# An adaLN transformer block, forward and backward: the work between the two attention loops rearranged (memory sides, halves of the dense gradient, column sums, operand loads)

## Chip, core and metric

The program runs on one core of a Trainium2 chip. The metric is device time in microseconds: the median of three runs of the kernel before is 2784.3 us (2782.75 to 2784.43). A profile records one execution by itself.

## What is computed

One transformer block with adaptive layer norm on x of 2048 tokens by 512 (bf16), its output, and the gradients of nine inputs for a given grad_out:

```python
mod = (_silu(c) @ w_mod).reshape(c.shape[0], 6, 1, -1)
sa, ca, ga, sb, cb, gb = (mod[:, i] for i in range(6))
h = _layernorm(x) * (1 + ca) + sa
x = x + ga * A(h, A_wqkv, A_wo)              # 32 heads of 16, softmax attention
h = _layernorm(x) * (1 + cb) + sb
x = x + gb * B(h, B_w1, B_b1, B_w2, B_b2)    # relu(h w1 + b1)^2 w2 + b2, width 1792
out, vjp = jax.vjp(f, A_x, A_wqkv, A_wo, B_w1, B_b1, B_w2, B_b2, c, w_mod)
return out, *vjp(grad_out)
```

The second line is written shorter here than in the reference.

## The kernel before

Tokens lie in 16 tiles of 128 (TT) or four chunks of 512 (QC); the dense width of 1792 in 14 blocks of 128 (FC) or four quarters of 448 (QF). The queues named SP, ACT and POOL issue DMAs in the order in which their instructions stand; a tile framework decides where each instruction is placed, under data dependences and the buffers of its pools. Products on PE are chained by hand (`pe`), some POOL instructions too (`chain("pool", ...)`). The stages:

- **Start (0 to about 109 us).** Loads of x (SP), wqkv, w_mod (ACT); layer norm; 16 DMA transposes make h1T (L164); q, k, v are projected tile by tile (L236) and stored to scratch memory: `qp_st` and `kp_st` (L251), `va_st` (L255), while POOL makes h1 and stores `h_st`. `prep_weights` (L334) transposes wo, w1 and w2 by DMA into `woT` and two `wbig` tiles and stores these as `w1T_st` and `w2T_st` for later reloads. The pool `wbig` has two buffers of 1792 KB; it is opened after the start's own pools are released.
- **Forward attention (to about 1100 us).** Scores, exponentials on ScalarE (L682) and products with v. Between them a generator `mlp(c, ...)` runs the MLP of chunk c, forward and backward: output projection, second layer norm, `h2T`, first dense layer into `rT` and its square `sT`; token-major copies `tokh` by DMA transposes; gradient of w2 (L486, sums over chunks in `dw2acc`); the dense gradient `ds` from w2T and `gfT` (grad_out transposed, times the gate gb) into `rT`; its transposes, stored to `dztok_st` (L514); gradient of the norm's input `dh` (L525) and the chain through the norm on VectorE and ScalarE (L531 to L555); column sums `sums` on POOL (L537, L538, L557, L611); per token tile the attention's output gradient (L578), stored for the loop, and the block's output (L604).
- **Tail (1100 to 1311 us).** Chunk 3 of the MLP. Wherever it calls `pump(k)`, k pieces of another generator, `fill`, are put in: gradients of wo and of w1 for quarters 0 and 1 (L779), by four-matmul groups, with two PSUM banks `ab0` and `ab1` and four `do` banks. The pieces need dz (the dense gradient, token-major), reloaded by `load_dz`.
- **A phase of its own (about 1251 to 1311).** The pool `bwdw` is opened, weights for the end are transposed (`wqT`), a third of w_mod is loaded, then the other two (`wmod2`); `ops` tiles for the backward loop are zeroed and their 28 loads issued (`load_one`, L905 and L909); gradients of w1 for quarters 2 and 3 (L933, L950) with dz2 and dz3; column sums multiplied out (L940); `mod_grads` for rows 2 to 5.
- **Backward attention loop (1311 to about 2652).** Eight groups of four heads; VectorE L999, ScalarE L985 and L1034, PE L981, L993, L1030, L1042, L1050, L1071.
- **Last stage (to 2769).** dq, dk, dv are turned into dx (L1202, `ln_back`), and the gradient of wqkv (L1211); token-major copies `dtok` come by 12 SP transposes (L1144); `flush_rows` sums rows by PE (L1194); `mod_grads` for rows 0 and 1; outputs go out on SP through `wqblk` (L1216) and `dwmod_sb` (L869).

`mod_grads(pool, wm, j0, j1, part)` makes, for each quarter of the rows of w_mod, one ScalarE product into `dwmod_sb` (one buffer, sent out on SP) and one VectorE product with its sum.

Of the kernel before, what the change touches and what calls it, by code (L numbers as in the profile page):

```python
# [17 lines left out]
BF = dt.bfloat16  # L18
# [15 lines left out]
def kernel(  # L34
# [52 lines left out]
    dcpart = persist.tile([P, 2, DC], F32, name="dcpart")  # L87
# [34 lines left out]
    SP.dma_start(out=wqkv_nat[:], in_=A_wqkv.rearrange("(ic p) j -> p ic j", p=P))  # L122
# [184 lines left out]
    with ExitStack() as ph:  # L307
        wbig = ph.enter_context(tc.tile_pool(name="fwb", bufs=2))
        onb = ph.enter_context(tc.tile_pool(name="f0", bufs=1))
        wkb = ph.enter_context(tc.tile_pool(name="fw0", bufs=2))  # L310

# [51 lines left out]
        def mlp(c, bank, tail=None):  # L363
# [74 lines left out]
            pump(14)  # L438
            for ic in range(DC):
# [11 lines left out]
            for fc in range(FC):  # L451
# [16 lines left out]
                if 2 <= fc < 6:  # L468
                    oc = fc - 2
                    DVE.tensor_scalar(gfT[:, oc, :], gfT[:, oc, :], modcol[:, 5, oc:oc + 1], None, ALU.mult)  # L470
# [4 lines left out]
            pb = bank()  # L475
            for t in range(4):
                pe(PE.matmul(pb[:], ones_bf[:, 0:P], gc[:, t, :], start=(t == 0), stop=(t == 3)))
            if c == 0:
                DVE.tensor_copy(db2acc[:], pb[0:1, :])
            else:  # L480
                DVE.tensor_tensor(db2acc[:], db2acc[:], pb[0:1, :], ALU.add)
            yield
            for fc in range(FC):
                pw = bank()
                for t in range(4):
                    pe(PE.matmul(pw[:], stok[fc // 7][:, t, (fc % 7) * P:(fc % 7 + 1) * P], gc[:, t, :],  # L486
                                 start=(t == 0), stop=(t == 3)))
                if c == 0:
                    DVE.tensor_copy(dw2acc[:, fc, :], pw[:])
                else:  # L490
                    DVE.tensor_tensor(dw2acc[:, fc, :], dw2acc[:, fc, :], pw[:], ALU.add)
                if c == QC - 1:
                    w2blk = wk.tile([P, D], BF, name="w2blk", tag="wb")
                    DVE.tensor_tensor(w2blk[:], dw2acc[:, fc, :], gb_bc, ALU.mult)
                    ACT.dma_start(out=out_6[fc * P:(fc + 1) * P, :], in_=w2blk[:])
                yield

            for fc in range(FC):
                pds = bank()
                for oc in range(DC):  # L500
                    pe(PE.matmul(pds[:], w2T[:, oc * FF + fc * P:oc * FF + (fc + 1) * P], gfT[:, oc, :],
                                 start=(oc == 0), stop=(oc == DC - 1)))
                db1p = wk.tile([P, 1], F32, name="db1p", tag="db1p")
                DVE.scalar_tensor_tensor(out=rT[:, fc, :], in0=pds[:], scalar=2.0, in1=rT[:, fc, :],
                                         op0=ALU.mult, op1=ALU.mult, accum_out=db1p[:])
                DVE.tensor_tensor(db1acc[:, fc:fc + 1], db1acc[:, fc:fc + 1], db1p[:], ALU.add)
                j = fc % 7
                if j == 0:
# [772 lines left out]
```

## Time and profile before

| what | value |
|---|---|
| median of three runs | 2784.3 us |
| the profiled execution | 2770.57 us |
| its span, first to last instruction | 2768.8 us |
| granted TensorE clock, mean | 0.922 of full |
| busy PE, DVE, ACT, POOL | 2270.3, 1838.4, 2275.3, 625.2 us |
| DMA | 466.89 MB, 169 GB/s mean |

Busy us by stage (windows of the trace):

| window | PE | DVE | ACT | POOL | clock | DMA share |
|---|---|---|---|---|---|---|
| 0 to 60 | 22.2 | 32.9 | 19.8 | 43.1 | 0.86 | 0.71 |
| 60 to 120 | 51.8 | 37.0 | 40.0 | 31.5 | 0.94 | 0.96 |
| 200 to 1085 | 719.7 | 368.6 | 854.7 | 169.6 | 0.86 | 0.44 |
| 1100 to 1250 | 119.7 | 82.2 | 25.6 | 37.0 | 0.83 to 0.93 | 0.52 to 1.10 |
| 1250 to 1311 | 32.2 | 24.1 | 9.6 | 24.0 | 0.78 | 0.86 |
| 1311 to 2652 | 1152.5 | 1215.3 | 1217.4 | 285.1 | 0.98 | 0.99 |
| 2652 to 2769 | 97.0 | 54.5 | 21.7 | 22.8 | 0.91 | 0.72 |

A row reads: of the window's length so many microseconds the engine was busy. A clock under 1 means that TensorE was granted less than full speed. A DMA share near 1 means that all 16 DMA engines moved packets all the time.

### The profile page before, as it was taken

To read this page: it belongs to the slowest core of one execution; us is meant where nothing else is said; L and a number is where in the kernel's file an instruction comes from. 1 tells how busy PE (TensorE), PEld (TensorE's weight loads), DVE (VectorE), ACT (ScalarE), POOL (GpSimd) and SP (SyncE) were. 2 spreads that over 40 slices of the span, in tenths; PEclk is the share of its full clock that TensorE was granted. 3 is DMA by queue.
4 is the path that set the end of the run, shared out by engine and by line. 5 is a ranking of instruction groups with operands and counts; after the bars stand their busy time and mean duration, and the time that the engine had idled before them with its cause. 6 is when DMAs were issued, how large, how long until landed. Compare 5 with 4: busy or idle time off the path is not lost. (4 is left out here: it accounts for less than half of the span.)

```text
span 2768.8 us, 48464 instructions
## 1 busy us (share of the span) xinstructions
PE 2270.3 (82%) x18161; PEld 780.1 (28%) x18265; DVE 1838.4 (66%) x2401; ACT 2275.3 (82%) x2891; POOL 625.2 (23%) x875
## 2 busy tenths in 40 slices
PE   4888879877877887875988888888888888888878
PEld 2322323222322322332222222222222222222233
DVE  5533334525442452653899999999999999999945
ACT  3789999999999998211899999999999999999922
POOL 7311110320140032043121212213122121211221
PEclk8989869978985997987899999999999999999999
DMA  7942243554444455598999999999999999999995
GB/s 198 209 126 62 69 147 92 136 162 106 117 122 127 96 160 182 121 182 205 177 205 189 202 199 195 204 195 207 191 202 201 194 209 189 205 196 191 182 258 137
DMA packets 1273298, 466.89 MB, mean 169 GB/s; under 512 B 1220387, under 2 KB 1242534, under 8 KB 1271270
## 3 DMA queue, kind: packets, MB, share of 16 engines
q1 hardware_dynamic: 1228916, 342.74, 61.6%
q0 software_dynamic: 34288, 109.23, 12.8%
q10 hardware_dynamic: 9858, 11.80, 1.3%
q8 instruction: 144, 2.36, 0.4%
q14 instruction: 92, 0.75, 0.1%
HBM read 116.46 MB, written 70.99 MB: 68 GB/s over the span
## 5 line engine op out<-in xcount | busy, mean ns | idle before, releaser
L999 DVE TENSOR_TENSOR dS_u<-psD_u,E_u 128x1024 bf16<-128x1024 f32 x1024 | 1215.1, 1221 | 120.0 <-PE psD_u L993 91.2
L985 ACT ACTIVATE E_u<-psS_u 128x1024 bf16<-128x1024 f32 x1024 | 1028.6, 1033 | 58.2 <-PE psS_u L981 50.3
L682 ACT ACTIVATE ET<-sbank 128x1024 bf16<-128x1024 f32 x1024 | 949.1, 1097 | 39.9 <-PE sbank L679 37.5
L993 PE MATMUL psD_u<-iv,ido 32*128 32x512 bf16 x2048 | 405.2, 385 | 183.0 <-ACT E_u L985 157.6
L1050 PE MATMUL accVK<-dS_u,sq 128*32 128x512 bf16 x2048 | 408.1, 395 | 0.5 <-DVE dS_u L999 0.5
L981 PE MATMUL psS_u<-ik,iq 32*128 32x512 bf16 x2048 | 403.0, 390 | 5.2 <-ACT w1blk L955 3.0
L1042 PE MATMUL accVK<-E_u,sdo 128*32 128x512 bf16 x2048 | 396.3, 395 | 0.0
L679 PE MATMUL sbank<-qt_sb,kt_sb 32*128 32x512 bf16 x2048 | 233.2, 441 | 86.9 <-ACT ET L682 72.2
L689 PE MATMUL oacc<-ET,va 128*32 128x512 bf16 x2048 | 234.3, 446 | 51.6 <-ACT ET L682 46.1
L993 PEld LDWEIGHTS <-ido 32*128 32x128 bf16 x2048 | 162.8, 91 | 373.1 <-issue 371.7
L1034 ACT ACTIVATE dST<-dSt 128x256 bf16<-128x256 bf16 x512 | 186.0, 392 | 29.6 <-PE dSt L1030 29.5
L1071 PE MATMUL accQ<-dST,sk 128*32 128x512 bf16 x2048 | 188.2, 388 | 1.0 <-ACT dST L1034 1.0
L1086 POOL TENSOR_TENSOR dQacc<-dQpart,dQacc 128x512 f32<-128x512 f32 x64 | 81.1, 1267 | 464.1 <-ACT dQpart L1084 464.1
L981 PEld LDWEIGHTS <-iq 32*128 32x128 bf16 x2048 | 99.9, 91 | 294.3 <-issue 268.2
L1042 PEld LDWEIGHTS <-sdo 128*32 128x32 bf16 x2048 | 97.4, 93 | 230.4 <-issue 230.4
L679 PEld LDWEIGHTS <-kt_sb 32*128 32x128 bf16 x2048 | 80.7, 93 | 225.0 <-issue 212.5
L689 PEld LDWEIGHTS <-va 128*32 128x32 bf16 x2048 | 66.7, 95 | 248.9 <-issue 248.6
L277 PE MATMUL xb<-h1T,wpadT 128*128 128x512 bf16 x338 | 97.2, 399 | 18.3 <-DVE pst L650 9.6
L695 DVE COPY ostage<-oacc 128x512 f32<-128x512 f32 x32 | 22.0, 687 | 135.9 <-PE oacc L689 135.9
L1030 PE MATMUL dSt<-identb,dS_u 128*128 128x128 bf16 x1024 | 102.1, 222 | 1.2 <-ACT dQpart L1084 0.7
L1091 POOL TENSOR_TENSOR dQstage<-dQpart,dQacc 128x512 bf16<-128x512 f32 x32 | 40.5, 1266 | 269.5 <-ACT dQpart L1084 269.5
L1050 PEld LDWEIGHTS <-sq 128*32 128x32 bf16 x2048 | 98.9, 93 | 8.6 <-issue 8.5
(261 smaller groups left out, 2365.9 us busy)
## 6 DMA issues: line engine op xcount, KB each, us to landing
wbig<-in_B_w_dram POOLq DMA_DIRECT2D x8, 1792.0 KB, 9.9
kt_sb<-KtP SPq DMA_DIRECT2D x24, 512.0 KB, 3.7
va<-va_st SPq DMA_DIRECT2D x32, 336.0 KB, 4.5
dST<-dS_u SPq DMA_TRANSPOSE x512, 3.9
wbig<-w2T_st POOLq DMA_DIRECT2D x4, 1792.0 KB, 14.6
wbig<-w1T_st POOLq DMA_DIRECT2D x4, 1792.0 KB, 8.5
dztok_st<-tokh POOLq DMA_DIRECT2D x8, 896.0 KB, 5.0
dqT<-dT_st SPq DMA_DIRECT2D x12, 512.0 KB, 6.3
```

The lines of the kernel that those rows point to most:

```text
L679: pe(PE.matmul(pair_ps[hq // 2][:, hq % 2, :], kt_sb[r:r + 32, kt * P:(kt + 1) * P], qt_sb[r:r + 32, :], start=True, stop=True, tile_posit ...
L682: ACT.activation(ET_t[u][:, 2 * pair:2 * pair + 2, :], pair_ps[pair][:], AF.Exp, scale=SCALE)
L689: pe(PE.matmul(oacc[32 * hq:32 * hq + 32, :], lhsT, ET_t[u][:, hq, :], start=(kt == 0), stop=(kt == TT - 1), tile_position=(0, 32 * hq), s ...
L981: pe(PE.matmul(ps[:, hi, :], L["iq"][r:r + 32, qt * P:(qt + 1) * P], L["ik"][r:r + 32, kc4 * 512:(kc4 + 1) * 512], start=True, stop=True, ...
L985: ACT.activation(E_t[s][:], ps[:], AF.Exp, scale=SCALE)
L993: pe(PE.matmul(ps[:, hi, :], L["ido"][r:r + 32, qt * P:(qt + 1) * P], L["iv"][r:r + 32, kc4 * 512:(kc4 + 1) * 512], start=True, stop=True, ...
L999: DVE.tensor_tensor(dS_t[s], ps[:], E_t[s][:], ALU.mult)
L1030: pe(PE.transpose(pt[:, j, :], src[:, (8 + j) * P:(9 + j) * P], identb[:]))
L1034: ACT.activation(dST_t[g][:, 3, 8 + 2 * j:10 + 2 * j, :], pt[:, 2 * j:2 * j + 2, :], AF.Identity)
L1042: pe(PE.matmul(accVK[r:r + 32, :], loads[hg]["sdo"][:, qt, r:r + 32], E_t[s][:, hi, :], start=(qt == 0), stop=False, tile_position=(0, r), ...
L1050: pe(PE.matmul(accVK[r:r + 32, :], loads[hg]["sq"][:, qt, r:r + 32], dS_t[s][:, hi, :], start=False, stop=(qt == TT - 1), tile_position=(0 ...
L1071: pe(PE.matmul(accQ[r:r + 32, :], L["sk"][:, kc4 * 4 + kt, r:r + 32], dST_t[g][:, :, hq * 4 + kt, :], start=(kt == 0), stop=(kt == 3), til ...
```

## The change

- The pools `onb`, `wkb` and `wbig` are opened at the very beginning on the right side of the memory, `carry` on the left; `wqkv_nat` takes one `wbig` buffer. The working pools of the MLP can be released inside the tail, and the loop's pools (`bwdw`, `strm`) opened there: the 28 loads, the zeroing of `ops` and the `wqT` transposes are issued behind the last output stores, ahead of the last pieces of `fill`.
- `gc` (grad_out of the chunk) is multiplied by the gate on VectorE, and `gfT` transposed from it; `gc` is loaded again before the output product. The gradient of w2 then needs no product by the gate.
- Gradient of w2 and dense gradient run in halves of seven blocks. The tail keeps both halves of dz in memory (`tokh`) and stores none; dz of the first 12 token tiles is loaded into the memory of `dw2acc` (`load1`), of `dzq`, and of a `wbig` tile (`load3`).
- In the tail, column sums are made by PE (`late_rows`) into one bank, the one that was `ab0`. Four `grad_o` go ahead of four `final_out`.
- All w1 gradients are in `fill`; quarters 2 and 3 use the four `do` banks.
- `mod_grads` for rows 2 and 3, and 4 and 5, are two calls in the last stage, with their parts of w_mod loaded one after the other into one buffer.

The order of instructions on SP's queue, by the built programs: before, the 16 transposes of h1T, all stores of the projection, then the 14 transposes of w1 and the store `w1T_st`; after, five transposes of w1, the 16 of h1T, nine of w1, `w1T_st`, then the stores of the projection. In the last stage the output of the first new `mod_grads` stands behind the 12 `dtok` transposes.

```diff
+    onb = tc.alloc_tile_pool(name="f0", bufs=1, side="right")
+    wkb = tc.alloc_tile_pool(name="fw0", bufs=2, side="right")
+    wbig = tc.alloc_tile_pool(name="fwb", bufs=2, side="right")
     fl = tc.alloc_tile_pool(name="fl", bufs=2, side="right")
     fe = tc.alloc_tile_pool(name="fe", bufs=3, side="right")
-    carry = tc.alloc_tile_pool(name="carry", bufs=1, side="right")
+    carry = tc.alloc_tile_pool(name="carry", bufs=1)
...
-    wqkv_nat = x0pool.tile([P, DC, 3 * D], BF, name="wqkv_nat")
+    wqkv_nat = wbig.tile([P, FC * D], BF, name="wbig", tag="wbig")
+    wqkv_nat = wqkv_nat[:, 0:DC * 3 * D].rearrange("p (ic j) -> p ic j", ic=DC)
...
-        wbig = ph.enter_context(tc.tile_pool(name="fwb", bufs=2))
-        onb = ph.enter_context(tc.tile_pool(name="f0", bufs=1))
-        wkb = ph.enter_context(tc.tile_pool(name="fw0", bufs=2))
...
-            for oc in range(DC):
-                SP.dma_start(out=gfT[:, oc, :], in_=grad_out[0][c * 512:(c + 1) * 512, oc * P:(oc + 1) * P],
-                             transpose=True)
+            for t in range(4):
+                DVE.tensor_tensor(gc[:, t, :], gc[:, t, :], gb_bc, ALU.mult)
+                SP.dma_start(out=gfT[:, :, t * P:(t + 1) * P], in_=gc[:, t, :], transpose=True)
...
+            for half in range(2):
+                for fc in range(7 * half, 7 * half + 7):
+                    pw = bank()
+                    for t in range(4):
+                        pe(PE.matmul(pw[:], stok[half][:, t, (fc - 7 * half) * P:(fc - 7 * half + 1) * P], gc[:, t, :],
+                                     start=(t == 0), stop=(t == 3)))
+                    if c == 0:
+                        DVE.tensor_copy(dw2acc[:, fc, :], pw[:])
+                    elif c < QC - 1:
+                        DVE.tensor_tensor(dw2acc[:, fc, :], dw2acc[:, fc, :], pw[:], ALU.add)
+                    else:
+                        w2blk = wk.tile([P, D], BF, name="w2blk", tag="wb")
+                        DVE.tensor_tensor(w2blk[:], dw2acc[:, fc, :], pw[:], ALU.add)
+                        ACT.dma_start(out=out_6[fc * P:(fc + 1) * P, :], in_=w2blk[:])
+                    yield
+                if half == 1:
+                    chain("pool", POOL.dma_start(out=gc[:], in_=g_dram[:, ts, :]))
+                    if tail:
+                        tail["load1"]()
...
+                    j = fc % 7
+                    SP.dma_start(out=tok[:, :, j * P:(j + 1) * P], in_=rT[:, fc, :], transpose=True)
+                    if j == 6:
+                        if tail:
+                            tail["dz"].append(tok)
+                        else:
+                            POOL.dma_start(out=dztok_st[:, ts, (fc - 6) * P:(fc + 1) * P], in_=tok[:])
...
+                if tail:
+                    tail["late_rows"]()
...
-                POOL.tensor_tensor(sums[:, 0, :], sums[:, 0, :], dxn2[:], ALU.add)
-                POOL.tensor_tensor(sums[:, 1, :], sums[:, 1, :], prod2[:], ALU.add)
+                if not tail:
+                    POOL.tensor_tensor(sums[:, 0, :], sums[:, 0, :], dxn2[:], ALU.add)
+                    POOL.tensor_tensor(sums[:, 1, :], sums[:, 1, :], prod2[:], ALU.add)
...
+                    tail["rows"] += [(0, t, dxn2), (1, t, prod2), (2, t, proda)]
+                else:
+                    POOL.tensor_tensor(sums[:, 2, :], sums[:, 2, :], proda[:], ALU.add)
+                pump(6 if t == 0 else 4)
...
+            if tail:
+                dOT2 = tTp.tile([P, 2, HG, P], BF, name="tT", tag="tT")
+            for t in range(4):
+                grad_o(t)
+                pump(4)
                 yield
-            late[0]()
+                if not tail:
+                    yield from final_out(t)
+                    yield
+            late.pop()()
+            if tail:
+                for t in range(4):
+                    yield from final_out(t)
+                    pump(1)
+                tail["late_rows"]()
...
+            def load1():
+                v = dw2acc.rearrange("p f d -> p (f d)")[:].bitcast(BF)[:, 0:T3 * QF]
+                dzq[1] = v.rearrange("p (t f) -> p t f", t=T3)
+                chain("pool", POOL.dma_start(out=dzq[1], in_=dztok_st[:, 0:T3, QF:2 * QF]))
+
+            def load3():
+                v = wbig.tile([P, FC * D], BF, name="wbig", tag="wbig")
+                dzq[3] = v[:, 0:T3 * QF].rearrange("p (t f) -> p t f", t=T3)
+                chain("pool", POOL.dma_start(out=dzq[3], in_=dztok_st[:, 0:T3, 3 * QF:4 * QF]))
+
+            pads2 = O_c[QC % 2].rearrange("p a d -> p (a d)").rearrange("p (i g c) -> p i g c", i=2, g=HG)
+            chain("pool", POOL.memset(O_c[QC % 2][:], 0.0))
+            tail = {"pads": [(dOpad[0][:], dOpad[1][:]), (pads2[:, 0], pads2[:, 1])], "h2r": h2r, "dz": [], "OT": OT3, "rows": [], "load1": load1, "load3": load3}
+
+            def late_rows():
+                for j, t, x in tail["rows"]:
+                    pe(PE.matmul(tail["sm"][32 * j:32 * j + 32, :], ones_bf[:, 0:32], x[:], start=(t == 0), stop=(t == 3),
+                                 tile_position=(0, 32 * j), skip_group_check=True))
+                tail["rows"].clear()
...
+                tail["sm"] = psY.tile([P, 512], F32, name="ab", tag="ab0")
+                for q in range(2):
+                    for ic in range(2 if q == 0 else 0, DC):
+                        acc = psY.tile([P, 512], F32, name="ab", tag="ab1")
+                        w1_tail(acc, q, ic, True)
                         yield
-                    four(acc, QF, h2_at(T3, ic), lambda j: tail["dz"][0][:, j, 0:QF], False, True)
-                    put_w1(acc, 0, ic)
-                    yield
-                dzq.append(load_dz(2))
+                        for c in range(QC - 1):
+                            w1_part(acc, q, ic, c, False, c == QC - 2)
+                            if c == QC - 2:
+                                put_w1(acc, q, ic)
+                            yield
+                    if q == 0:
+                        t_ = fillr.tile([P, T3, QF], BF, name="dzq", tag="dzq")
+                        chain("pool", POOL.dma_start(out=t_[:], in_=dztok_st[:, 0:T3, 2 * QF:3 * QF]))
+                        dzq[2] = t_
...
+                accs = {}
+                for q in (2, 3):
+                    for ic in range(DC):
+                        accs[q, ic] = psY.tile([P, 512], F32, name="do", tag=f"do{ic}")
+                        w1_tail(accs[q, ic], q, ic, True)
                         yield
+                    if q == 3:
+                        tail["tok_done"] = True
+                    for ic in range(DC):
+                        for c in range(QC - 1):
+                            w1_part(accs[q, ic], q, ic, c, False, c == QC - 2)
+                            if c == QC - 2:
+                                put_w1(accs[q, ic], q, ic)
+                            yield
...
+            for j in range(4):
+                DVE.tensor_tensor(sums[32 * j:32 * j + 1, j, :], sums[32 * j:32 * j + 1, j, :],
+                                  tail["sm"][32 * j:32 * j + 1, :], ALU.add)
...
+            while "tok_done" not in tail:
+                next(filling)
+            tTp.release()
+            wk.release()
+            one.release()
+
+            bwdw = tc.alloc_tile_pool(name="bwdw", bufs=1)
+            dmodbc = bwdw.tile([P, 6, D], BF, name="dmodbc")
+            wqT = bwdw.tile([P, 12, D], BF, name="wqT")
+            wmod_v = w_mod.rearrange("(ic p) j -> p ic j", p=P)
+            wmod_cur = []
+
+            def load_wmod(i):
+                if i is not None:
+                    wmod_cur.append(bwdw.tile([P, DC, 2 * D], BF, name="wmod", tag="wmod"))
+                    ACT.dma_start(out=wmod_cur[-1][:], in_=wmod_v[:, :, 2 * i * D:(2 * i + 2) * D])
+                return wmod_cur[-1]
...
+            load_wmod(1)
+            strm = tc.alloc_tile_pool(name="phIs", bufs=2)
+            ops = {nm: [strm.tile([P, n], BF, name=f"{nm}{i}", bufs=1) for i in range(2)]
+                   for nm in ("iq", "ik", "ido", "iv")}
+            for nm in ("iq", "ik", "ido", "iv"):
+                DVE.memset(ops[nm][0][:], 0.0)
...
+            for i in range(len(LOADS)):
+                load_one(0, i)
+            for nm in ("iq", "ik", "ido", "iv"):
+                chain("pool", POOL.memset(ops[nm][1][:], 0.0))
+            for jb in range(12):
+                SP.dma_start(out=wqT[:, jb, :], in_=A_wqkv[:, jb * P:(jb + 1) * P], transpose=True)
...
+            for j, row in ((0, 3), (1, 4), (2, 2), (3, 5)):
+                pr = ybank()
+                pe(PE.matmul(pr[:], onesf[:], sums[:, j, :], start=True, stop=True))
+                if row in (3, 4):
+                    DVE.tensor_tensor(dmodbc[:, row, :], pr[:], cbr[:], ALU.mult)
+                else:
+                    DVE.tensor_copy(dmodbc[:, row, :], pr[:])
+            for _ in filling:
...
+        mod_grads(wk, load_wmod(None), 2, 4, 1)
+        wmod = load_wmod(2)
...
-                ln_back(t0 + i, pds[i])
+                done = ln_back(t0 + i, pds[i])
+            if t0 == 0:
+                mod_grads(wk, wmod, 4, 6, 2, done)
+                wmod = load_wmod(0)
```

More of the change, by code (lines that the diff above doesn't have):

```diff
@@ L498, in mlp @@
[L498 to L508, printed above, removed]
-                    tok = wk.tile([P, 4, 7 * P], BF, name="tokh", tag="tokh")
-                SP.dma_start(out=tok[:, :, j * P:(j + 1) * P], in_=rT[:, fc, :], transpose=True)
-                if tail and j == 0:
-                    tail["dz"].append(tok)
-                if j == 6:
-                    POOL.dma_start(out=dztok_st[:, ts, (fc - 6) * P:(fc + 1) * P], in_=tok[:])
-                yield
+            if not tail:
+                db2_part()
+                yield
@@ L561, in mlp @@
             if tail:
-                dzq1 = wbig.tile([P, FC * D], BF, name="wbig", tag="wbig")
-                dzq1 = dzq1.rearrange("p (t f) -> p t f", t=TT)
-                POOL.dma_start(out=dzq1, in_=dztok_st[:, :, QF:2 * QF])
-                tail["dzq1"] = dzq1
                 tail["od"] = (Oc, dac)
-                pump(6)
+                tail["load3"]()
+                pump(8)
+                tail["late_rows"]()
             else:
@@ L768 @@
             ACT.dma_start(out=h2r[:, 0:T3, :], in_=h2_st[:, 0:T3, :])
-            dzq = [load_dz(0)]
-            tail = {"h2r": h2r, "dz": [], "OT": OT3}
             nb = [0]
@@ new lines @@
+            for nm in ("iq", "ik", "ido", "iv"):
+                DVE.memset(ops[nm][0][:], 0.0)
+            steps = [(hg, kc4, qt, pr) for hg in range(HG) for kc4 in range(QC) for qt in range(TT) for pr in range(2)]
+            NS = len(steps)
+            BLK = 2 * TT
+            GRP = 8
+            loads = {}
+            LOADS = [(nm, src, j) for nm, src in (("iq", QtP), ("ik", KtP), ("ido", dOtP), ("iv", VtP))
+                     for j in range(4)]
+            LOADS += [(nm, src, 4 + j) for nm, src in (("sdo", dop_st), ("sq", qp_st), ("sk", kp_st)) for j in range(4)]
@@ L961 @@
[L961 to L962 removed]
+    for pool in (fillr, wbig, wkb, onb, keep):
+        pool.release()
     with ExitStack() as ph:
```

250 lines of the change are left out of this document (93 added, 157 removed).

## Prediction

> **What bounds the kernel now.** I began with the rows of busy time by stage. The attention stages before 1100 us and from 1311 to 2652 us are bound by ScalarE and VectorE (2652 less 1311 is 1341 us, of which each is busy some 1216), and the change leaves their loops alone. Between them lies the tail that the change rewrites, 211 us long. Its rows of 20 us, from which I quote four (window, its length, then busy us and instructions of PE, PEld, DVE, ACT, POOL; then granted clock, DMA share, GB/s):
>
> ```profile
> 1180.00:1200.00 20.00, 18.91 (x92) 8.97 (x92) 8.39 (x22) 2.96 (x5) 6.95 (x7) 1.00 1.79 183
> 1200.00:1220.00 20.00, 6.45 (x14) 1.97 (x14) 11.63 (x24) 2.49 (x4) 11.27 (x10) 0.57 0.72 216
> 1260.00:1280.00 20.00, 9.21 (x29) 3.73 (x27) 6.74 (x7) 1.46 (x2) 12.16 (x24) 0.74 1.17 198
> 1280.00:1300.00 20.00, 6.18 (x22) 2.67 (x23) 8.08 (x8) 7.18 (x5) 3.12 (x6) 0.57 0.76 299
> ```
>
> TensorE does the work of this stage and has three holes; over all 211 us it is busy 151.9 and idle 59.1. No other engine is busy for more than 107, so the tail is TensorE plus its waits. The timeline of TensorE after the last token product (start, length; the bracket is the wait ahead of it):
>
> ```profile
> 1251.60 9.24 PE L933 MATMUL gb<-dzq,h2r 128*128 128x448 bf16 x48 [1.43 <-issue]
> 1260.68 3.60 PE L940 MATMUL gb<-sums,onesf 128*128 128x512 f32 x8
> 1273.89 4.94 PE L950 MATMUL gb<-dz,h2r 128*128 128x448 bf16 x16 [9.61 <-issue]
> 1285.52 0.93 PE L950 MATMUL gb<-dz,h2r 128*128 128x448 bf16 x2 [6.70 <-DMA dz<-dztok_st]
> 1294.74 13.46 PE L950 MATMUL gb<-dz,h2r 128*128 128x448 bf16 x62 [8.29 <-DVE w1blk L957]
> 1311.17 0.40 PE L981 MATMUL psS_u<-ik,iq 32*128 32x512 bf16 x4 [2.97 <-ACT w1blk L955]
> ```
>
> It waits for operands that are asked for only in this phase. The list of waits in the tail names the hole at 1200 (waiter, what ended the wait; total, times, longest):
>
> ```profile
> POOL dztok_st L514 <- DMA tokh<-rT: 47.7, 2, 34.7
> PE do L779 <- DVE ac L555: 13.9, 3, 6.0
> DVE proda L554 <- POOL sums L557: 7.1, 1, 7.1
> PE xb L486 <- DVE dw2acc L491: 7.1, 4, 6.5
> ```
>
> POOL, in order, is stuck on storing tokh until its transposes have landed; the sums behind it are late, VectorE waits for the buffer that they read, and TensorE for VectorE. Last I read the queue of SP at the start, because the instruction order of the changed kernel differs there:
>
> ```profile
> 26.73 21.98 SPq L164 DMA_TRANSPOSE h1T<-x_tok  x16
> 54.31 0.41 SPq L251 DMA_DIRECT2D qp_st<-tokpad  x1
> 111.19 19.24 SPq L339 DMA_TRANSPOSE wbig<-in_B_w_dram  x14
> ```
>
> and ScalarE's in the last stage:
>
> ```profile
> 2702.95 1.33 ACT L1180 ACTIVATE tqa<-x0J,c2a 128x512 bf16<-128x512 bf16 x2 [10.52 <-DVE c1a L1176]
> 2707.74 1.33 ACT L1180 ACTIVATE tqa<-x0J,c2a 128x512 bf16<-128x512 bf16 x2 [3.45 <-DVE c1a L1176]
> ```
>
> **The tail, part by part.**
>
> *The separate phase of 1250 to 1311 dissolves.* Its waits, 1.4 + 9.6 + 6.7 + 8.3 + 3.0 = 29.0 us, go: dz2, dz3, wmod2 and the loop's operands are now asked for earlier, and the q=2 and q=3 gradients of w1 run inside the tail. The 16 matmuls at 1273.89 took 0.309 us each against 0.217 in the run of 62 (13.46 / 62): at full clock 1.5 us less, and by the same comparison some 2 us less for the eight matmuls in 1194 to 1216 (3.8 us). Together -3.5.
>
> *Operands exposed.* The loop needs the first 16 of 28 loads; POOL issued these from 1260.86 to 1273.51, 12.7 us. They now start behind the last output stores, some 3.5 us after the last token product (four VectorE and POOL steps of under 1 us), and land some 5 us after issue (the 5.0 of the stores of dztok in the list of DMA issues; loads here are quoted between 3.7 and 14.6). Beside them lie 64 matmuls at 0.208 (13.3) and the f32 sums (3.6), 16.9. So 3.5 + 12.7 + 5 - 16.9 = +4.3; 0 if the loads land in 3.7 and the stores go sooner, +11 if the landing takes 12. I take 4.3. The wqT transposes lie behind these in time and gate nothing until the last stage. Memsets on DVE (four, about 0.9) run while TensorE has this work.
>
> *Column sums.* POOL's 16 adds (1.15 us) become 16 matmuls of 0.227, +3.6 on TensorE. The wait of 13.9 goes with POOL's 7.1 and with the store of tokh that the tail no longer makes; but part of it is VectorE's chain for a token tile (some 6 us from dxn to ac), so between -7.1 and -13.9. The pump now gives 4 to 6 pieces a tile to fill that, so I take -12.
>
> *One bank fewer.* The sums hold ab0, so six w1 groups in ab1 wait for their eviction, 0.54 us a time (L783): +3.2, with 0 and +7 as bounds (0 if the pump puts other work there, twice as much if an output buffer is late).
>
> *Halves of the dense gradient.* The same 56 + 56 matmuls in another order. Evicting dw2 now needs a free w2blk buffer, so the wait of 6.5 us behind the 1792 KB load of w1T stays: 0, bounds -6 and +6. The gate product on gc (four of about 0.42) sits ahead of four SP transposes of gfT that came straight from DRAM before; ten or more us of fill cover them. With that cover gone TensorE would be 6.7 us late (four transposes of 1.25 and the products). The db2 product slides into an idle stretch (-1.3), and the shorter dz traffic and small waits after 1215 give some -3. The reload of gc is next read for the output product (1228 in before, where the w2 gradient ends at 1164).
>
> Sum of the tail: -29.0 - 3.5 + 4.3 + 3.6 - 12 + 3.2 - 1.3 - 3 = **-37.7 us** (ends -24 and -52).
>
> In the three earlier chunks the gc reload and the products lie under ScalarE, which is busy 855 of 885 us from 200 to 1085: 0, bounds -2 and +4.
>
> **The start.** A second wbig buffer is now free from the beginning, so the scheduler places the 14 transposes of B_w1 earlier on SP's queue: five ahead of h1T, nine and the store w1T_st ahead of the first qp_st. One takes 19.24 / 14 = 1.37 us. In before SP idled from 23.4 to 26.7, so five of them (6.9) delay h1T by 3.5. The 16 h1T transposes then end at 52.3, nine more at 64.6; w1T_st waits for the last to land (2.5), and the first qp_st is issued near 67.5 instead of 54.3: +13. All of phase B is queued behind it: TensorE, through two token buffers. From 60 to 100 the DMA share is 1.04 at 238 to 250 GB/s, so the 1.79 MB of w1T_st push the remaining stores another 7.3 us. Some 2 us come back because POOL's h_st stores use the blocked stretch; and from 110 to 150 ScalarE is idle 7 us, most of it behind the same transposes and store that no longer run there: -6. So +13 + 7.3 - 2 - 6 = **+12** (ends +3, if phase B's pace elsewhere leaves slack, and +34, below).
>
> [...]
>
> **The last stage.** Mod gradients for rows 2 to 5, once a call with 4 DVE products (2.29) and 4 ACT products (2.0) in the tail, become two calls here: 8 DVE products of 1.22 and 8 ACT products of 1.07. The first call falls into a stretch where both engines wait for dqT. The second does not: its dwmod_sb has one buffer, freed when the first call's output has left, and that output stands on SP behind all 12 dtok transposes (to 2720). So ScalarE, which reaches the second call after the tqa of about 2704, waits to some 2726 (2720 and 6 us for 1 MB), then spends 4.3 us; the last six tqa come at 2731 instead of 2707 to 2718. Behind them VectorE's ten-odd us of rows t=10 to 15, plus four products of 1.22, end near 2745 instead of 2729, and TensorE's row sums at 2733 wait about 10 us for prod. Later output evictions have 7.8 us of slack on ScalarE. **+10** (ends 0, if TensorE's 138 matmuls find other work and the closing drain absorbs it, and +20, if it adds the closing dwmod chain too). The extra 4 MB (17 us at 245 GB/s) fit into the stage's 28% of idle DMA.
>
> **Sum:** -37.7 + 12 + 10 = -15.7 us. Against the profiled execution (span 2768.8, time 2770.57) that is 2754.9; the runs shown have a median 13.7 us above it, so I carry the difference to the median: 2784.3 - 15.7 = **2769**, with 2756 to 2779 as its own range.
>
> **Rivals.**
>
> 1. *SP's queue at the start decides; slower.* If the 14 transposes run beside the loads of x and w_mod at the pace of woT's four, 2.36 us each (14.00 to 23.44), they take 33, with landing and store 43 us, less 3.3 idle and 6 regained: +34. With the rest, -37.7 + 34 + 10 = +6: 2790. For: DMA moves 350 GB/s at 10 to 20 us. Against: 172 GB/s at 20 to 30, and the 14 ran at 1.37 at share 0.75. It decides when the start costs more than 27.7.
>
> 2. *The shifts at start and end are absorbed.* Phase B's waits give back most (+3) and the closing chain has slack (0): -34.7, 2750. For: ScalarE idles at both ends. Against: DMA is full there.
>
> 3. *It doesn't do what it says: operands still come last.* POOL needed 23.9 us for all 28 issues, and several of them waited for earlier loads to land. If the first product waits for all (3.5 + 23.9 + 5 - 16.9 = 15.5 exposed, not 4.3) and one more small wait appears, the tail gives some -25: 2781.
>
> **How the numbers follow.** Forecast 0.50, rival 1 0.20, rival 2 0.20, rival 3 0.10. About 0.2% (5.6 us) is what a measurement of this kernel can tell from no change. Faster: 0.47 of the forecast, 0.20 of rival 2, 0.01 of rival 3, 0.68. Same: 0.03 and 0.07, 0.10. Slower: rival 1 and the bad ends of rival 3, 0.22. The range runs from some way below rival 2 to just above rival 1, 2744 to 2796.
>
> **What would show it.** In the changed profile: first qp_st near 67 and KtP stores near 123 confirm the start; a first exp delayed less than 6 us refutes it. No wait of TensorE on ac over 3 us near 1200, and a first loop product some 26 us earlier (1311 less 37.7 plus 12 is 1285). A ScalarE wait of some 20 us before dwmod_sb in the last stage, and a wait of some 10 before prow. I am wrong if the loads stand in front of the loop for over 15 us, if halves leave w2blk waits over 12, or if the span from the loop's last product to the end stays at 117.

## The result, and the profile after

The changed kernel takes 2848.49 us (median of 4 runs, 2835.25 to 2858.85) against 2783.53 for the one before beside it: ratio 1.024, 95% interval 1.0212 to 1.0268. It is 65 us slower; 15.7 us faster was forecast. One profiled execution of each, cut at the last exponential of forward attention, the first product of the backward loop, and the first product of the last stage (us):

| stage | before | after | difference | forecast |
|---|---|---|---|---|
| start and forward attention | 1099.5 | 1107.5 | +8.0 | +12 |
| tail | 211.7 | 197.2 | -14.5 | -37.7 |
| backward loop | 1344.3 | 1404.4 | +60.1 | 0 |
| last stage | 113.3 | 132.7 | +19.4 | +10 |
| span | 2768.8 | 2841.8 | +73.0 | -15.7 |

The loop, in which the change touches no instruction, decides. Two windows of 1200 us in it, the kernel before and then the changed one (window, its length, busy us and instructions of PE, PEld, DVE, ACT, POOL; clock, DMA share, GB/s):

```profile
1400.00:2600.00 1200.00, 1032.03 (x10170) 324.37 (x10171) 1096.83 (x925) 1097.06 (x1532) 256.91 (x397) 0.99 1.00 198
```

```profile
1400.00:2600.00 1200.00, 1031.97 (x9675) 319.69 (x9672) 1046.20 (x880) 1051.53 (x1457) 244.06 (x380) 0.93 1.12 189
```

VectorE gets through 880 products instead of 925. The DMA share is higher (1.12 against 1.00) and less is moved (189 against 198 GB/s): a packet takes longer. The share adds up the times of the packets. It reaches 1.79 in a row of the tail before, so packets overlap, and a share of 1.00 does not say that the engines were full. The DMA queue that carries the transposes, and their issue and landing, before:

```profile
q1 hardware_dynamic: 844492, 212.45, 91.5%
...
dST<-dS_u SPq DMA_TRANSPOSE x464, 4.0
```

and after, with the waits of the loop below (waiter, releaser; total us, times, longest):

```profile
q1 hardware_dynamic: 801393, 201.62, 101.5%
...
dST<-dS_u SPq DMA_TRANSPOSE x441, 5.2
```

```profile
ACT E_u L1040 <- PE psD_u L1048: 40.0, 43, 3.3
DVE dS_u L1054 <- DMA dST<-dS_u: 36.4, 28, 5.5
PE psS_u L1036 <- DVE dS_u L1054: 29.7, 54, 2.9
```

Before, 91.5% of 16 engines for 1200 us over 844,492 packets (252 bytes on average) are 20.8 ns per packet; after, 24.3. A transpose lands 5.2 us after its issue, not 4.0, so the buffer of dS_u comes free late, and VectorE waits for it: a wait that is 36.4 us in this window and that the list before does not have. ScalarE and TensorE wait in a ring behind.

The granted clock fell too, from 0.99 to 0.93. Here is a stretch of 100 us before, then three of the changed kernel:

```profile
2311.00:2411.00 100.00, 86.06 (x854) 27.04 (x853) 91.64 (x79) 91.96 (x129) 21.74 (x38) 1.00 1.01 199
```

```profile
2205.00:2305.00 100.00, 87.66 (x816) 27.23 (x817) 87.93 (x75) 88.20 (x122) 23.09 (x41) 0.92 1.15 196
2305.00:2405.00 100.00, 86.25 (x852) 27.38 (x844) 91.04 (x77) 91.55 (x128) 18.36 (x28) 0.99 1.11 186
2405.00:2505.00 100.00, 85.21 (x774) 26.14 (x772) 83.60 (x71) 84.64 (x117) 24.55 (x37) 0.90 1.15 192
```

In the second of the three, TensorE and VectorE do about as much as before, although the DMA share is 1.11: slower packets alone do not slow every stretch. Over the whole window of 1200 us VectorE is busy 50.6 us less than before. Cut into 60 pieces of 20 us, 45 of these lie in the 22 pieces whose clock is below 0.97, and 20 of these 22 hold a wait of VectorE or TensorE for a transpose, or come right behind a piece that does. The timeline around one such wait shows the order: TensorE waits 1.1 us for a transpose up to 1542.8 and VectorE 3.3 us up to 1546.0; from the first of these to about 1559 the loop's pairs of products on TensorE take 0.61 us, not 0.39; the granted clock is 0.50 there (1542.8 to 1559) and 1.00 from 1500 to 1530. So a late transpose seems to cost the wait and then a stretch in which TensorE is slower. This is read from the order of events; no run separates the two shares.

The tail shows what was forecast and two things that were not. Its last products on TensorE, and the waits:

```profile
1270.68 3.20 PE L835 MATMUL do<-tokh,h2r 128*128 128x448 bf16 x16
1273.72 0.92 PE L835 MATMUL do<-wbig,h2r 128*128 128x448 bf16 x4
1274.47 1.88 PE L994 MATMUL xb<-sums,onesf 128*128 128x512 f32 x4
1291.25 3.75 PE L994 MATMUL xb<-sums,onesf 128*128 128x512 f32 x4 [14.90 <-DVE dmodbc L996]
1294.80 9.22 PE L835 MATMUL do<-wbig,h2r 128*128 128x448 bf16 x44
1304.65 0.40 PE L1036 MATMUL psS_u<-ik,iq 32*128 32x512 bf16 x4 [0.63 <-ACT ostage L839]
```

```profile
ACT ostage L839 <- DMA out_dram<-ostage: 18.0, 3, 10.4
...
DVE w2blk L499 <- DMA out_dram<-w2blk: 12.6, 6, 7.6
```

The holes for POOL's sums and for dz have gone. A new one of 14.9 us stands where the loop's memory is taken over, and evictions wait for output buffers (ostage 18.0, w2blk 12.6).

The queue of SP at the start is as forecast, with the first qp_st at 66.55 (54.31 before):

```profile
23.73 6.51 SPq L339 DMA_TRANSPOSE wbig<-in_B_w_dram  x5
30.36 21.80 SPq L168 DMA_TRANSPOSE h1T<-x_tok  x16
52.22 11.67 SPq L339 DMA_TRANSPOSE wbig<-in_B_w_dram  x9
66.07 0.38 SPq L340 DMA_DIRECT2D w1T_st<-wbig  x1
66.55 0.37 SPq L255 DMA_DIRECT2D qp_st<-tokpad  x1
```

and so is the wait of ScalarE in the last stage:

```profile
2791.96 4.27 ACT L1008 ACTIVATE dwmod_sb<-dmodbc,silucol 128x1024 bf16<-128x1024 bf16 x4 [17.88 <-DMA out_dram<-dwmod_sb]
```

### The profile page after: what moved, and what is told of

It is laid out like the page before. It is cut to its first block, busy times and chain, and to the rows that moved or that the text cites. A ratio compares the mean times of both kernels' runs of the same rounds, so it can differ in the third digit from the quotient of the medians.

```text
span 2841.8 us, 48599 instructions
## 1 busy us (share of the span) xinstructions
PE 2339.6 (82%) x18281; PEld 794.0 (28%) x18281; DVE 1831.3 (64%) x2396; ACT 2287.0 (80%) x2899; POOL 611.2 (22%) x864
## 4 chain that ended last, share of the span: by engine, by line
PE 15%; ACT 14%; DVE 10%; DMA 8%; issue 4%; SPq 3%; POOL 1%; DVEq 0%; ACTq 0%; POOLq 0%
ACT E_u L1040 11%; DVE dS_u L1054 9%; DMA dST<-dS_u 7%; PE psD_u L1048 4%; PE psS_u L1036 4%; PE accVK L1097 4%; ACT dST L1089 2%; SPq L1199 2%; PE accQ L1126 2%; PE dSt L1085 1%; DMA out_dram<-wqblk 1%; DMA dT_st<-dQstage 0%; POOL dT_st L1068 0%; SPq L986 0%; DMA ik<-KtP 0%
## 5 line engine op out<-in xcount | busy, mean ns | idle before, releaser
L1048 PE MATMUL psD_u<-iv,ido 32*128 32x512 bf16 x2048 | 422.5, 402 | 150.7 <-ACT E_u L1040 137.3
L1036 PE MATMUL psS_u<-ik,iq 32*128 32x512 bf16 x2048 | 420.2, 406 | 35.4 <-DVE dS_u L1054 31.5
L1105 PE MATMUL accVK<-dS_u,sq 128*32 128x512 bf16 x2048 | 424.6, 411 | 0.5 <-DVE dS_u L1054 0.5
L1097 PE MATMUL accVK<-E_u,sdo 128*32 128x512 bf16 x2048 | 411.9, 411 | 0.3
L1126 PE MATMUL accQ<-dST,sk 128*32 128x512 bf16 x2048 | 200.4, 412 | 10.7 <-DMA dST<-dS_u 9.5
## 6 DMA issues: line engine op xcount, KB each, us to landing
wbig<-w2T_st POOLq DMA_DIRECT2D x4, 1792.0 KB, 14.9
```

The lines of the kernel that those rows point to most:

```text
L1036: pe(PE.matmul(ps[:, hi, :], L["iq"][r:r + 32, qt * P:(qt + 1) * P], L["ik"][r:r + 32, kc4 * 512:(kc4 + 1) * 512], start=True, stop=True, ...
L1048: pe(PE.matmul(ps[:, hi, :], L["ido"][r:r + 32, qt * P:(qt + 1) * P], L["iv"][r:r + 32, kc4 * 512:(kc4 + 1) * 512], start=True, stop=True, ...
L1097: pe(PE.matmul(accVK[r:r + 32, :], loads[hg]["sdo"][:, qt, r:r + 32], E_t[s][:, hi, :], start=(qt == 0), stop=False, tile_position=(0, r), ...
L1105: pe(PE.matmul(accVK[r:r + 32, :], loads[hg]["sq"][:, qt, r:r + 32], dS_t[s][:, hi, :], start=False, stop=(qt == TT - 1), tile_position=(0 ...
L1126: pe(PE.matmul(accQ[r:r + 32, :], L["sk"][:, kc4 * 4 + kt, r:r + 32], dST_t[g][:, :, hq * 4 + kt, :], start=(kt == 0), stop=(kt == 3), til ...
```

## Experiments

**Why is the loop slower?** The diff has one line that looks like bookkeeping: `dcpart` in the pool that is opened first grows from 32 to 48 bytes a partition. In the built programs the loop's tiles, which lie behind it on the left, start 32 bytes later than before (bytes in a partition, first buffer):

```
             before   after
dS_u         123136   123168     = 481 x 256, and 32 past it
dST          143616   143648     = 561 x 256, and 32 past it
```

dS_u is the source of the loop's transposes and dST their destination. Theory A is that the 32 bytes slow them; theory B is the new side of the memory or the neighbours. Four kernels tell these apart.

```diff
 # e1_after_aligned, on the changed kernel
-    dcpart = persist.tile([P, 3, DC], F32, name="dcpart")
+    dcpart = persist.tile([P, 6, DC], F32, name="dcpart")
```

> The changed kernel with dcpart padded from 48 to 96 bytes a partition, so that every tile allocated behind it on the left (the operands of the backward loop among them: dS_u, dST) starts at a multiple of 64 bytes as in the kernel before; the changed kernel has them at 32 past one. Theory A (a start 32 bytes off makes the loop's DMA transposes slower: per packet 24.3 ns of DMA engine in the loop against 20.8): the loop goes back from 1404 us (first loop product to first product of the last stage) to some 1344, the DMA share in it from 1.11 to 1.00, and the time to about 2785. Theory B (the loop is slower for another reason, such as the side of memory on which its tiles lie or what else runs beside it): no change, about 2848.

```diff
 # e2_before_shifted, on the kernel before
-    dcpart = persist.tile([P, 2, DC], F32, name="dcpart")
+    dcpart = persist.tile([P, 3, DC], F32, name="dcpart")
```

> The kernel before with dcpart one row larger (48 bytes for 32) and nothing else: all later tiles on the left move by 32 bytes. Theory A: the loop slows by some 60 us, the last stage by a few, to about 2845. Theory B: 2784, no change.

```diff
 # e3_source_shifted, on the kernel before: ahead of dS_u, and likewise ahead of dST in its pool
+            if s == 0:
+                DVE.memset(ework.tile([P, 8], F32, name="padS", bufs=1)[:], 0.0)
             if pr == 0:
                 dS_q[s // 2] = ework.tile([P, 4, 512], BF, name="dS_u", tag="dS_u", bufs=5)
```

> The kernel before with a tile of 32 bytes ahead of dS_u and one behind it: the sources of the loop's transposes start 32 bytes past a multiple of 64, their destinations dST at a multiple. Theory A1 (the writes into dST are what is slower): no change, 2784. Theory A2 (the reads of dS_u are slower): about 2840. Theory B: no change in this and the next.

e4_dest_shifted has the second of these two tiles alone.

> The kernel before with a tile of 32 bytes ahead of dST alone: the destinations start 32 bytes past a multiple of 64, the sources dS_u at a multiple (dQacc and the stages behind dST move too). A1 (writes): about 2840. A2 (reads): 2784.

| run | dS_u past a multiple of 256 | dST | time us | ratio (95%) | loop us | ns per packet |
|---|---|---|---|---|---|---|
| before | 0 | 0 | 2773 to 2784 | | 1344.3 | 20.8 |
| changed | 32 | 32 | 2848.5 | 1.024 (1.0212 to 1.0268) | 1404.4 | 24.3 |
| e1 | 64 | 64 | 2833.8 | 1.0214 (1.0193 to 1.0236) | 1402.5 | 24.2 |
| e2 | 32 | 32 | 2843.2 | 1.0248 (1.0205 to 1.0291) | 1409.8 | 24.2 |
| e3 | 32 | 64 | 2823.5 | 1.0171 (1.0135 to 1.0206) | 1397.1 | 24.2 |
| e4 | 0 | 32 | 2775.9 | 1.0004 (0.9992 to 1.0015) | 1344.5 | 21.0 |
| e5 | 0 | 0 | 2777.2 | 1.0012 (0.9995 to 1.0029) | 1344.4 | 21.1 |
| e6 | 128 | 128 | 2823.8 | 1.0178 (1.0149 to 1.0208) | 1400.2 | 24.3 |

e2 settles theory B: sixteen bytes of scratch, with nothing else changed, cost the kernel before 2.5%. e3 and e4 put it on the source: with the destination at 32, e2 and the changed kernel, whose source is at 32 too, are slow, and e4, whose source is at 0, is not; and e3 is slow with every tile ahead of dS_u at its place. e1 failed as a repair, and by that told more: a multiple of 64 is as bad as 32, so the first idea of the boundary was too small. e5 (the changed kernel at a multiple of 256) and e6 (the kernel before at 128) followed.

```diff
 # e5_after_aligned256, on the changed kernel
-    dcpart = persist.tile([P, 3, DC], F32, name="dcpart")
+    dcpart = persist.tile([P, 18, DC], F32, name="dcpart")
 # e6_source_shifted128, on the kernel before, ahead of dS_u
+                DVE.memset(ework.tile([P, 32], F32, name="padS", bufs=1)[:], 0.0)
```

> The changed kernel with dcpart padded to 288 bytes: dS_u then starts at a multiple of 256 bytes, as in the kernel before (e1 had it at a multiple of 64 but not of 128, and was as slow as the changed kernel). Theory A2 with a boundary of 128 bytes or more (a source that starts off that boundary makes the loop's transposes slower): loop back from some 1404 to 1344 us, last stage some 5 faster, about 2782 against the changed kernel's 2848, and some 10 us above the kernel before at most. Theory C (the loop is slow for what the changed kernel does elsewhere, and e2 and e3 for another reason): about 2835 as e1.

> The kernel before with a tile of 128 bytes ahead of dS_u: sources at 128 past a multiple of 256. If a start at a multiple of 128 is enough: no change, loop 1344 us. If it has to be 256 or more: loop some 1400 us, time about 2830.

Both decide for 256. The loop of e5, windows and queue as above:

```profile
1400.00:2600.00 1200.00, 1030.93 (x10168) 324.01 (x10167) 1097.67 (x925) 1096.07 (x1529) 255.96 (x397) 0.99 1.01 198
```

```profile
q1 hardware_dynamic: 843362, 212.17, 92.6%
...
dST<-dS_u SPq DMA_TRANSPOSE x463, 3.8
```

It is the loop of before again: 925 products, clock 0.99, share 1.01, 198 GB/s, landing in 3.8.

**What do the three priced steps cost?** On e5, which stands level with before, one repair after the other was added.

```diff
 # e7_db2: on e5
-            db2bf = wk.tile([1, D], BF, name="db2bf", tag="wb")
+            db2bf = onb.tile([1, D], BF, name="db2bf")
 # e8_db2_j: on e7
-        SP.dma_start(out=out9_v[:, :, j0 * D:j1 * D], in_=ob[:])
+        ACT.dma_start(out=out9_v[:, :, j0 * D:j1 * D], in_=ob[:])
 # e9_all: on e8; last_store is the store of KtP[0], tr each of the 14 transposes of w1
+                issue_order(tr, last_store)
```

> As e5, with db2bf in a pool of its own, so that zeroing iq, which takes over the old memory, no longer waits for the store of db2bf, that stands behind six wqT transposes on SP. If this store holds the loop's loads: the wait of TensorE of 14.9 us at the end of the tail shrinks to 5 to 8, the loop starts 7 to 9 us earlier, and the time is some 8 us under e5. If the hole has another cause (the wqT transposes, the last output): no change against e5.

> As e7, with the outputs of mod_grads issued by ScalarE's queue and not by SP's. If the place behind the dtok transposes is what holds ScalarE (17.9 us before dwmod_sb) and with it the rows t=10 to 15 and TensorE: that wait goes, and the last stage is 8 to 14 us shorter. If the stage is long for the extra 4 MB or the 8 products alone: within 3 us of e7.

> As e8, with the 14 transposes of w1 ordered behind the last store of the projection, as in the kernel before. If the start costs what the place on SP's queue costs: the first exp some 14 us and the end of forward attention some 8 us earlier, 8 us under e8, and with all four repairs about 2784 - 25 = 2750 to 2760. If forward attention is held by something else: no change against e8.

| run | time us | ratio (95%) | start and forward | tail | loop | last stage |
|---|---|---|---|---|---|---|
| e5 | 2777.2 | 1.0012 (0.9995 to 1.0029) | 1106.0 | 196.5 | 1344.4 | 126.0 |
| e7 | 2773.1 | 0.9986 (0.9973 to 0.9999) | 1105.2 | 191.3 | 1344.4 | 128.9 |
| e8 | 2769.6 | 0.9979 (0.9967 to 0.9990) | 1106.3 | 190.4 | 1344.5 | 126.0 |
| e9 | 2755.5 | 0.9933 (0.9912 to 0.9953) | 1087.8 | 196.7 | 1343.7 | 125.5 |
| e10 | 2756.3 | 0.9939 (0.9916 to 0.9963) | 1095.3 | 197.2 | 1344.5 | 124.0 |
| e11 | 2747.5 | 0.9913 (0.9881 to 0.9944) | 1088.5 | 186.7 | 1346.0 | 120.7 |
| e11 again | 2747.4 | 0.9906 (0.9877 to 0.9935) | 1088.0 | 185.8 | 1344.3 | 125.4 |
| e12 | 2747.5 | 0.9905 (0.9885 to 0.9925) | 1095.2 | 190.9 | 1343.1 | 116.3 |
| e13 | 2757.5 | 0.9946 (0.9923 to 0.9968) | 1092.8 | 202.5 | 1344.7 | 115.3 |
| e14 | 2751.7 | 0.9911 (0.9886 to 0.9936) | 1091.6 | 188.3 | 1344.4 | 119.2 |

The stages come from one execution each. The tails of e9, e10, e12 and e13, with the same code there, run from 190.9 to 202.5, so 5 us in a tail prove little.

The place on SP's queue at the start is shown: e9 issues its first qp_st at 54.3 and ends forward attention 18 us before e8, and the time falls by 14. e8 refuted the mechanism given for the last stage. Its ScalarE no longer waits late in the stage: the second call's products come 24 us into it, and the wait ahead of them holds nothing up, since the next work of ScalarE waits for VectorE anyway:

```profile
2665.37 4.27 ACT L1008 ACTIVATE dwmod_sb<-dmodbc,silucol 128x1024 bf16<-128x1024 bf16 x4 [12.34 <-DMA out_dram<-dwmod_sb]
```

and the stage is as long as in e5, 2.9 us shorter than in e7, where 8 to 14 were expected. e7's gain is small, 4 us with intervals that overlap. In the changed kernel VectorE waited for the store of db2bf, which stood behind six transposes; in e7 and e9 it waits some 5 us for something else:

```profile
1282.51 0.91 DVE L957 MEMSET iq<- 128x1024 uint32 x1 [8.14 <-DMA out_dram<-db2bf]
```

```profile
1262.64 0.91 DVE L958 MEMSET iq<- 128x1024 uint32 x1 [5.07 <-DMA wqT<-in_A_wqkv_dram]
```

(the changed kernel, then e9). The releaser named in e9 is inferred; the landing of the last store of outq, issued 7 us earlier, was the other candidate. e11 tried it, on top of e10, which moved transfers of the last stage.

```diff
 # e10_j_dma_late: on e9; first output and next load on SP behind the last dtok transpose,
 # the second call moved behind the last tqa
+        mod_grads(wk, load_wmod(None), 2, 4, 1, last_dt)
+        wmod = load_wmod(2, last_dt)
...
+            if t3 == 0:
+                mod_grads(wk, wmod, 4, 6, 2, after=done[0])
+                wmod = load_wmod(0)
 # e11_tail: on e10; the rest of fill also goes ahead of the four f32 sums
-                outq = wk.tile([P, D], BF, name="outq", tag="wa")
+                outq = Oc[:, t, :] if tail else wk.tile([P, D], BF, name="outq", tag="wa")[:]
```

> As e9, with the last stage's extra transfers put behind the 12 dtok transposes: the output of the first mod_grads and the load of the next part of w_mod go out on SP behind them, the second mod_grads runs behind the last tqa. The last stage of e9 takes 125.5 us against 113.3 before. Theory D (the DMA engines bound the stage up to its 85th us, share 1.0 to 1.2, and the 4 MB moved into that stretch cost their own time): 114 to 118 us, 8 to 11 under e9. Theory E (VectorE's and ScalarE's eight more products are what it costs): 122 to 126, no change.

> As e10, with the tail's last outputs outq written into the free O_c tile and not into the pool that is released, and the last w1 products ahead of the four f32 sums on TensorE. If zeroing iq waits for the landing of the last output store: it starts some 5 us earlier, the loads and the loop too, tail 197 to some 190, 5 to 8 us under e10. If it waits for something else: only the order on TensorE changes, 0 to 3 us.

In e11 the memset starts right behind VectorE's earlier work, with the wqT transposes still there, and the tails with this edit (e11 twice, e14) are 185.8 to 188.3:

```profile
1253.04 0.91 DVE L960 MEMSET iq<- 128x1024 uint32 x1 [0.29 <-issue]
```

So the last output store held the memset and the loop's loads behind it: opening the loop's memory in the tail was paid with the landing of the last transfer out of the old pools. How the gain of some 10 us divides between this and the new order on TensorE was not tried.

**The last stage's 12 us.** Theory D puts these on the extra bytes, theory E on the extra products. e10 moved the bytes and gained nothing: 124.0. It did get TensorE to the first product of dWqkv 10 us sooner (64.6 us into the stage against 74.7; 63.2 before), and then lost it: ScalarE waited 16.2 us for an output buffer of wqblk at the end (10.7 before). e12 and e13 leave out the bytes or the VectorE products, and so part of the gradients; e14 gives wqblk two more buffers and dx1t one fewer.

```diff
 # e12_no_dma: on e9, no output of rows 2 to 5, no load of the later parts
+        if j0 == 0:
             ACT.dma_start(out=out9_v[:, :, j0 * D:j1 * D], in_=ob[:])
 # e13_no_dcprod: on e9, the VectorE product only in the last call
+            if j0 == 0:
                 DVE.tensor_tensor_reduce(out=pm[:], in0=wm[:, ic, :], in1=dm, ...
 # e14_drain: on e11
-                wblk = wk.tile([P, D], BF, name="wqblk", tag="wqblk")
+                wblk = wk.tile([P, D], BF, name="wqblk", tag="wqblk", bufs=4)
```

> As e9 without the transfers that the change put into the last stage: no load of the second and third part of w_mod (the products read the first part again) and no output of the mod gradients for rows 2 to 5, 4 MB in all; that part of the outputs is not computed. Theory D (the extra bytes are what lengthens the last stage, wherever in it they stand): 125.5 us back to 113 to 117, time 8 to 12 under e9. Theory E (the extra products on VectorE and ScalarE): 122 to 126, within 4 of e9.

> As e9 without the eight VectorE products of the two moved calls (9.8 us of VectorE; the gradient of c lacks rows 2 to 5), all transfers and the ScalarE products kept. Theory E: last stage 114 to 118 us. Theory D: 122 to 126.

> As e11 with four buffers for wqblk and three for dx1t. In e10 the first product of the last weight gradient came 10 us earlier than in e9 (64.6 against 74.7 us after the first product of the stage), but the end only 1.5: ScalarE waited 16.2 us for a wqblk buffer behind an output of 1 MB. If that wait is what gave the gain back: last stage of 120.7 (e11) to some 113 to 116, time 5 to 8 under e11, about 2740. If the closing transfers themselves take that long: 120, within 3 of e11.

> e11 once more beside e14, so that the two are read on one chip: about 2747, last stage 120 to 124 us.

In the profiled executions the stage takes 116.3 without the bytes, 115.3 without the products and 125.5 with both, as if each alone fitted beside the rest. The medians bear this out for the bytes only: 2747.5 for e12 against 2755.5 for e9, while e13 is no faster with 2757.5 (its profiled execution spends 11 us more on the start and the tail, where the code is e9's). Two executions of e11 differ by 4.7 us in this stage. So the bytes seem to have a price (the intervals of the two ratios still overlap), and that of the products is not shown. e14 is inconclusive, 119.2 against 120.7 and 125.4 for e11, with the time no better; ScalarE waits 13.1 us with four buffers too, so two more buffers did not remove the closing wait. No kernel that was tried makes all the gradients here without the longer stage. e11, the fastest with the whole computation, is 0.9% faster than before.

## Why the prediction was wrong, by its steps

**The step that failed is in the prediction's first paragraph, on what bounds the kernel: "the change leaves their loops alone".** No instruction changed there and its price was put at nothing, but the loop's operands moved by 32 bytes. e2, e3 and e5, with e4 as the control, show that this is worth 53 to 65 us in the loop. The reading that the loop is "bound by ScalarE and VectorE" (1216 of 1341 us) left out that VectorE's buffers wait for their transposes. With 17% more time per packet these land in 5.2 us, not 4.0; VectorE stands still for 36.4 us in 1200, and the clock falls behind such waits (0.50 from 1542.8 to 1559, right behind one of them). No rival had it.

Sources at a multiple of 256 were fast (20.8 to 21.1 ns per packet); 32, 64 and 128 past one were slow alike, with 24.2 to 24.3, 24.2 and 24.3, at packets of 252 bytes on average. So over these three the cost does not rise with the distance. What makes it, no run shows.

**The tail**: -14.5 for -37.7; the mechanisms were right, the sizes were not. The 29 us of waits of the separate phase went, and so did the 13.9 for ac. But "Operands exposed" was priced as loads beside TensorE's work, 4.3 us, and the memsets on DVE, which "run while TensorE has this work", at nothing. In the run VectorE stood 8.1 us before the first memset; behind it are the reciprocal and dmodbc, whose PSUM banks TensorE needs for its third and fourth sum: 14.9. What was queued behind the waiting memset was not asked. The evictions of the single bank were put at +3.2; by the timeline TensorE waited 1.6, 6.6, 0.6 and 0.6 for ostage, 9.5 in all. Two loads of 1344 KB, issued at 1206.17 and 1215.44 and landed 20.3 and 15.3 us later, were under way at the longest of these, which ended at 1222.09 (that they cause it was not tried). TensorE's waits behind w2blk, put at no change from 6.5, were 7.2, 1.7 and 0.7. These three terms, 10.6, 6.3 and some 3 us over their prices, are 20 of the 23.2 that the tail fell short. VectorE's own waits for w2blk, 12.6, are just over the 12 at which the prediction said that it would be wrong.

**The start**: the first qp_st was forecast near 67 and came at 66.55. The store to KtP was issued at 122.92, not 106.34; of these 16.6 us 4.3 arose behind the first qp_st, where 7.3 less 2 were forecast. That the 1.79 MB of w1T_st push the stores was the author's estimate, and no run separates it. The price of the place on the queue is 18 us by e9 against e8, and 15 by the means (1106.2 for the five kernels with it, 1091.3 for the seven from e9 on), where +12 was forecast. Only +8.0 shows, since forward attention without it ends 4 to 12 us earlier than in the profile of before, and not later than in e3, e4 and e6 (1096.5 to 1103.8). That gain was put at 0 and was not taken apart.

**The last stage**: +19.4. It is 6.7 longer than in e5; eight of its dtok transposes take 40.5 us, for 32.5 before. How much of this the shifted sources cost is open: e1, shifted too, has 128.8, and e2 only 2.4 more than before. The 12.7 of e5 is near the +10 forecast, but the wait of ScalarE that gave the number is not what costs (e8), and that the extra 4 MB "fit into the stage's 28% of idle DMA" does not go with e12, which is 8 us faster without them: the idle DMA lies in the last 40 us, and the bytes come before (in e9 the DMA share is 1.00 to 1.23 from 12 to 82 us into the stage, with the new outputs of 1 MB issued there, and 0.15 to 0.38 behind that).

Of the rivals, the first saw the place, but its price stayed under the 27.7 from which it would decide. The second had it the other way: neither end absorbed its shift. The third has the size of the hole by luck, 15.5 for 14.9: the first product of the loop waited 0.6 us, and not for a load. Its time, nearly no change, is what is left once the sources are at their place: the stages other than the loop sum to +12.9, and e5 measures 1.0012.

## What to carry to other kernels

When the size of any early tile changes, compare where the later tiles start: here the sources of the loop's DMA transposes, moved to 32 or 128 bytes past a multiple of 256, cost the kernel before 1.7 to 2.5% (e2, e3, e6), and putting them back at a multiple took the changed kernel from 1.024 to 1.0012 (e5). A stage whose instructions are unchanged still has to be priced when its operands move and its buffers wait for DMA. When memory is handed over early, ask which transfer out of the old tiles lands last, and what is queued behind the instruction that waits for it.

## What the runs showed of the hardware

The loop's DMA transposes, which read from and write to on-chip memory, took 24.2 to 24.3 ns per packet in the five kernels whose sources start 32, 64 or 128 bytes past a multiple of 256, and 20.8 to 21.1 in before, e4 and e5, where they start at one; they landed in 5.0 to 5.2 us and in 3.8 to 4.0. With the source at a multiple, a destination 32 past one made no difference (e4, 21.0 ns). The granted TensorE clock from 1400 to 2600 us was 0.93 to 0.94 in the changed kernel, e3 and e6, and 0.99 in before, e4 and e5; over a whole profiled execution it was 0.889 to 0.904 in all five kernels with shifted sources and 0.922 to 0.928 in all the others. In the changed kernel 20 of the 22 pieces of 20 us with a clock below 0.97 hold a wait for a transpose or follow one that does; behind one such wait it was 0.50, from 1542.8 to 1559.
